# A gated linear attention with a cosine-gated MLP on one core: the last four first-layer tiles as three one-pass products

## The chip, the cores and the metric

The kernel runs on one core of one Trainium2 chip. The metric is the device time of one execution in microseconds; the median over runs is what counts. Five engines take part: TensorE (PE: matmuls, PEld: weight loads), VectorE (DVE), ScalarE (ACT), GpSimd (POOL) and SyncE (SP), which issues most DMAs.

## The reference

```python
# q, k, v, a_re, a_im: (4, 8, 768, 48);  w_in: (384, 2048);  w_out: (2048, 384)
mag = np.sqrt(a_re * a_re + a_im * a_im)
scale = np.minimum(mag, 0.999) / (mag + 1e-06)
a_re_n, a_im_n = (a_re * scale, a_im * scale)
for t in range(S):                      # a complex gate, one per head and channel
    new_re = ar * S_re - ai * S_im
    new_im = ar * S_im + ai * S_re
    S_re, S_im = (new_re + kv, new_im)  # kv: outer product of k and v of step t
    y[:, :, t] = np.einsum('bhd,bhde->bhe', q[:, :, t], S_re)
x = y.transpose(0, 2, 1, 3).reshape(3072, 384)
h = x @ w_in
out = (h * np.cos(h)) @ w_out
```

All of it is float32.

## The kernel before

The 3072 steps are 24 chunks of 128; two chunks make a group, so there are 12 groups (`NG`), three to a batch. `fast_path` turns the recurrence into sums within a chunk: logarithms of the gates are summed by a matmul (`lgs`, exponentials of which scale k and q), angles likewise (`phs`), and the scaled keys and queries are multiplied by cosine and sine of the phase. Scores (`sc`), masked by `causal` into `atm`, meet v and the state carried from the chunk before (`yp`); the state itself comes from `sp`. The result goes through DRAM and comes back as `xT`, 384 rows in three blocks by 256 steps.

For one group n the main loop hands these parts to `weave`, which sorts them by a place between 0 and 1 given with each part:

- `logs(n + 1)`: `log_steps`, ScalarE and VectorE in turn: squares of re and im, logarithms, exponentials, ending in `hi` and `lo`, the two halves of the logarithm that `lgs` multiplies (`prods`, `p_powers`).
- `chunks(n)`: `f_scores`, `f_state`, `f_out` for both chunks.
- `prods(n + 1)`: `lgs`, the arc tangent, `g_split` (a `lo` of the angle), `p_apply`.
- `products(n - 1, ...)`: the second layer of the group before. It is a 2x2 block product done with seven products instead of eight (`seventh`, Strassen's way in Winograd's form); `mixed` makes the four left-hand sums s1 to s4 from the gates, `quarters` those of w_out.
- `phases(n + 1)` and `keys(n + 1)`: `phs`, sine and cosine (`g_trig`), the four products into `ks` and `qs` (`g_stack`), and the turn of both (`f_transpose`): VectorE transposes 32x32 blocks into `tr`, SyncE moves them to DRAM (`moved`) and back (`kT`, `qT`).
- `first(n)`: the first layer, eight tiles of 256 hidden columns (`mm1`). A tile is six products of 128x128 weights by 256 steps in float32, each issued as two matmul rows; ScalarE then takes the sine of the sum (a cosine by its bias) and the square of the sum with its largest value kept (`junk`, a check for range), and VectorE multiplies sum and cosine (`gate`).

Everything on TensorE and most of ScalarE's functions stand in the order in which they are written (`chain` ties each to the one before; `behind` puts one instruction after another without a wait). The other instructions of VectorE, ScalarE and SyncE are placed by the scheduler of the Tile layer. PSUM has five buffers "a" and three for the layers: `hp`, the sum of a first-layer tile, takes "m", "m", "acc" in turn, which `op` and `sum` of the second layer use as well.

Products of two `float32r` operands are issued as one matmul row each, those of float32 as two. `upper_half` uses the type already for `lgs` and `phs`: `hi` by a copy to that type, `lo` by what is left.

Of the kernel before, what the change touches and what calls it, by code (L numbers as in the profile page):

```python
# [487 lines left out]
def fast_path(ctx, tc, q, k, v, a_re, a_im, moe_w_in, moe_w_out, out, least, odd, wide,  # L488
# [12 lines left out]
    G = 2  # L501
# [94 lines left out]
    w_in = wts.tile([C, DF // 256, ND, 256], F32)  # L596
# [4 lines left out]
    def weight_parts():  # L601
        wi = moe_w_in.rearrange("(c p) f -> p c f", p=C)
        wo = moe_w_out.rearrange("(j p) e -> p j e", p=C)
        return ([(w_in[:, i], wi[:, :, ts(i, W)]) for i in range(DF // W)],
                [(w_out[:, ds(j, 2)], wo[:, ds(j, 2)]) for j in range(0, NJ, 2)])
# [20 lines left out]
    def fetched(src):  # L626
        _, a, b = src.shape
        raw = stage["pool"].tile([C, a, b], I64, tag="raw", name="raw", bufs=stage["bufs"])
# [103 lines left out]
    def log_steps(g, i, n):  # L732
# [4 lines left out]
        if i == 0:  # L737
            if g == 0:
                x["sin"] = temp("tan", 2)
            for name in "lg", "tan", "rs", "mag":  # L740
                x[name] = temp(name, 2 if name == "tan" else 1)
        m2, sq, rs, mag = (cut(x[name], i, n) for name in ("lg", "tan", "rs", "mag"))
# [57 lines left out]
    def p_powers(g, i):  # L800

        x = X[g]
        if i == 0:
            x["P"], x["Q"] = x["lg"], temp("Q")
# [91 lines left out]
    def g_trig(g, i, n):  # L896
        x = X[g]
        if i == 0:
            x["cos"] = temp("rs")
            if g:  # L900
# [3 lines left out]
        vector.tensor_scalar(out=cs.bitcast(U32), in0=ph.bitcast(U32),  # L904
                                scalar1=0x7FFFFFFF, scalar2=None, op0=ALU.bitwise_and)
        special(out=sn, in_=ph, func=AF.Sin, scale=TWO_PI)
        special(out=cs, in_=cs, func=AF.Sin, scale=-TWO_PI, bias=half_pi_b)

    def g_stack(g, i, n):
        x = X[g]  # L910
        if i == 0:
            for name in "ks", "qs":
                x[name] = gt.tile([C, G * H, 2, D], F32, tag=name, name=name)
        for name, product in ("ks", "Q"), ("qs", "mag"):
            for a, trig in enumerate(("cos", "sin")):
                vector.tensor_tensor(
                    out=x[name][:, ds(i * H, n * H), a],
                    in0=cut(x[product], i, n).rearrange("p (x d) -> p x d", d=D),
                    in1=cut(x[trig], i, n).rearrange("p (x d) -> p x d", d=D), op=ALU.mult)

    def f_transpose(g, i, n, name):


        if i == 0:
            X[g][name] = ft.tile([D2, G * H, Q4, 32] if name == "kT" else [D2, Q4, G * H, 32], F32,
                                 tag=name, name=name, bufs=1)
        tr = ft.tile([C, NB, n * H, 32], F32, tag="tr", name="tr")
        turn = vector.transpose(out=tr, in_=X[g][name[0] + "s"][:, ds(i * H, n * H)].rearrange(
            "p x a d -> p x (a d)").rearrange("p x (r b) -> p b x r", b=NB))
        if name == "qT" and "gated" in X[g - 1]:  # L930
# [27 lines left out]
    def f_scores(n, hh):  # L958
        y = Y[n]
        if hh == 0:  # L960
            y["atm"] = ft.tile([C, H, C], F32, tag="atm", name="atm")
# [99 lines left out]
    def mm1_sums(g, jp, i=None):  # L1061
# [9 lines left out]
        ps = x["hp"][jp]  # L1071
        lo, n = (0, G) if i is None else (i, 1)
# [605 lines left out]
```

## Time and profile before

| | |
|---|---|
| time, median of 3 runs | 655.62 us (655.18 to 656.74) |
| span of the profiled execution | 651.2 us |
| the profiled execution's own time | the page gives the span alone; 4.4 us lie between it and the median |
| busy: PE, DVE, ACT, POOL | 641.0, 492.0, 392.8, 30.9 us |
| granted TensorE clock | 1.000 over the span |
| first-layer tiles, `hp` | 1176 matmul rows, 252.5 us busy |
| gate: sine, square, product | 96 each, 687, 591, 684 ns |
| DMA traffic | 94.90 MB, mean 146 GB/s |

In the rows of the profile L687 is the line of `matmul`, L676 that of the wrapper through which most VectorE and ScalarE calls go, L707 that of `special` (ScalarE functions with a table). In a timeline row stand start and duration in us, engine, line, operation, output<-inputs, shapes and count, and in brackets the idle time ahead with what ended it. In the chain of work each row is a start, a duration and what ran. Rows of TensorE end some time after the next begins, since matmuls overlap; the pace is read from starts.

### The profile page before, as it was taken

How to read it: one execution, taken by the hardware profiler on the slowest of the kernel's cores; microseconds unless marked ns; L12 is line 12 of the kernel's file. 1: busy time of each engine (PE TensorE's matmuls, PEld its weight loads, DVE VectorE, ACT ScalarE, POOL GpSimd, SP SyncE). 2: the span in 40 equal slices, each digit the busy share in tenths (PEclk: the TensorE clock that was granted, in tenths of full speed). 3: DMA queues.
4: the chain of work that ended last, by engine and by line, in shares of the span. 5: the costliest groups of instructions: out<-in, count | busy, mean ns of one | idle time of the engine just before them, and what ended most of it. 6: DMA issues, size and time to landing. Idle time of an engine off the chain costs nothing.

```text
span 651.2 us, 10758 instructions
## 1 busy us (share of the span) xinstructions
PE 641.0 (98%) x4075; PEld 576.4 (89%) x4075; DVE 492.0 (76%) x799; ACT 392.8 (60%) x726; POOL 30.9 (5%) x53
## 2 busy tenths in 40 slices
PE   8999999999999999999999999999999999999997
PEld 6888877777999999899899899899899999999996
DVE  6999989888687688786787787876877878862251
ACT  7898687284583593494494485485576476433330
POOL 4010200000000000010010010000000000000000
PEclk9999999999999999999999999999999999999999
DMA  9968755727627656747738737836836843363001
GB/s 249 244 179 203 225 164 123 170 62 182 146 49 182 158 146 148 194 110 167 209 82 191 204 85 167 205 96 151 226 105 146 219 123 98 112 134 120 25 1 31
DMA packets 232920, 94.90 MB, mean 146 GB/s; under 512 B 208701, under 2 KB 221246, under 8 KB 232858
## 3 DMA queue, kind: packets, MB, share of 16 engines
q1 hardware_dynamic: 225320, 68.51, 45.3%
q0 software_dynamic: 5824, 25.50, 11.7%
q8 instruction: 34, 0.56, 0.4%
q10 hardware_dynamic: 1714, 0.11, 0.2%
q14 instruction: 28, 0.23, 0.1%
HBM read 69.28 MB, written 24.81 MB: 144 GB/s over the span
## 4 chain that ended last, share of the span: by engine, by line
PE 92%; ACT 4%; DVE 3%; DMA 0%; issue 0%; SPq 0%; DVEq 0%
PE hp L687 38%; PE op L687 18%; PE sum L687 16%; PE sc L687 6%; PE yp L687 6%; PE sp L687 4%; PE phs L687 2%; PE lgs L687 1%; ACT tan L707 1%; PE yr L687 1%; PE tp L948 1%; ACT rs L707 1%; ACT lg L707 1%; ACT L703 1%; DVE mag L676 1%; DVE atm L676 1%
## 5 line engine op out<-in xcount | busy, mean ns | idle before, releaser
L687 PE MATMUL hp<-xT,w_in 128*128 128x256 f32 (+1 forms) x1176 | 252.5, 375 | 0.0
L687 PEld LDWEIGHTS hp<-xT,w_in 128*128 128x128 f32 x1176 | 219.6, 190 | 30.2 <-issue 0.2
L707 ACT ACTIVATE gate<-hp,half_pi_b 128x512 f32<-128x512 f32 x96 | 66.0, 687 | 118.5 <-PE hp L687 118.5
L687 PE MATMUL op<-w_out,gate 128*128 128x192 f32 (+1 forms) x448 | 100.7, 374 | 0.0
L676 DVE TENSOR_TENSOR gate<-hp,gate 128x512 f32<-128x512 f32 x96 | 65.7, 684 | 45.8 <-ACT junk L676 45.7
L687 PEld LDWEIGHTS op<-w_out,gate 128*128 128x128 f32 x448 | 75.9, 190 | 16.9 <-issue 2.0
L676 ACT ACTIVATE junk<-hp 128x512 bf16<-128x512 f32 x96 | 56.7, 591 | 0.0
L687 PE MATMUL sum<-t_s,s 128*128 128x192 f32 x320 | 56.3, 329 | 0.0
L687 PEld LDWEIGHTS sum<-t_s,s 128*128 128x128 f32 x320 | 52.1, 190 | 1.5 <-issue 1.5
L676 DVE TENSOR_TENSOR atm<-sc,causal 128x512 f32<-128x512 f32 x48 | 32.9, 689 | 23.4 <-PE sc L687 23.4
L687 PEld LDWEIGHTS sc<-qT,kT 96*128 96x128 f32 x384 | 47.4, 192 | 2.3 <-issue 0.6
L687 PE MATMUL sc<-qT,kT 96*128 96x128 f32 x384 | 49.0, 276 | 0.2 <-ACT qT L676 0.2
L676 ACT ACTIVATE ot<-sum 128x192 f32<-128x192 f32 x39 | 12.6, 322 | 53.7 <-PE sum L687 53.4
L676 DVE SCALAR_TENSOR_TENSOR ot<-op,ot 128x192 f32<-128x192 f32 x40 | 13.3, 354 | 38.0 <-PE op L687 36.4
L687 PE MATMUL yp<-atm,v 128*48 128x128 f32 x352 | 33.6, 277 | 0.9 <-ACT Q L707 0.6
L703 ACT ACT_TABLE_LOAD x24 | 30.8, 1283 | 1.2 <-PEq L1662 0.7
L676 ACT COPY yT<-yp 48x512 f32<-48x512 f32 x44 | 25.3, 574 | 7.4 <-PE yp L687 7.0
L687 PE MATMUL yp<-qT,state 96*48 96x128 f32 x304 | 29.7, 272 | 0.0
L687 PE MATMUL sum<-w_out,gate 128*128 128x192 f32 x160 | 29.7, 329 | 0.0
L687 PE MATMUL sp<-v,ks 128*96 128x48 f32 x320 | 29.7, 245 | 0.0
L687 PEld LDWEIGHTS sp<-v,ks 128*96 128x96 f32 x320 | 29.6, 165 | 0.0
L676 ACT CAST tan<-phs 128x384 int32<-128x384 f32 x24 | 11.4, 480 | 29.4 <-PE phs L687 29.4
(147 smaller groups left out, 987.4 us busy)
## 6 DMA issues: line engine op xcount, KB each, us to landing
moved<-tr SPq DMA_DIRECT2D x20, 768.0 KB
raw<-in_moe_w_in_dram POOLq DMA_DIRECT2D x16, 768.0 KB, 5.1
raw<-in_moe_w_out_dram POOLq DMA_DIRECT2D x16, 768.0 KB, 4.6
kT<-moved SPq DMA_DIRECT2D x40, 192.0 KB
qT<-moved SPq DMA_DIRECT2D x10, 768.0 KB
k<-in_k_dram SPq DMA_DIRECT2D x24, 192.0 KB
q<-in_q_dram SPq DMA_DIRECT2D x24, 192.0 KB
v<-in_v_dram SPq DMA_DIRECT2D x24, 192.0 KB
```

Of the source, the lines that this page charges most:

```text
L676: ins = getattr(self.engine, op)(**kw)
L687: chain(nc.tensor.matmul(out, **kw), "tensor")
L703: chain(nc.scalar.preload_act_table_set(table))
L707: chain(nc.scalar.activation(func=func, **kw))
L948: chain(nc.tensor.transpose(ps[:, h], X[g][name[0] + "s"][:, x0 + h].rearrange("p a d -> p (a d)"), ident), "tensor")
```

## The change

For four of the eight tiles of a group (jp = 4 from group 2 on, 5 and 6 from group 3, 7 from group 4) the six float32 products are replaced. Weights and x are cut into an upper part of 12 bits and a lower rest (scaled by 4096 for the weights): w = wh + wl, x = xh + xl. With a third pair, wx = wh - 4096 wl and xx = xh - 4096 xl in the terms of the code, three one-pass sums of six products each give the tile: wh xh and wl xl go into `hp`, wx xx into a second PSUM tile `hb` from pool "a". ScalarE copies `hb`, scaled, into the tile's gate buffer (`cross_out`), VectorE adds that into `hp` (`whole_sum`), and sine, square and product follow with a factor 1 + 1/4096. Per group x is cut by `x_halves` (`cut`, `xl`, `xx` on VectorE, `xh` on ScalarE), the weights once each by `halves`.

Other edits come with it: first-layer tiles run in the order 0 to 7 instead of 0, 4, 1, 5 and so on; `mixed` makes s1 alone, and s3, s2 and s4 are made later, in place in the gates, by `mixed_again`; the phases stand one product sooner; `g_trig` takes the absolute value on ScalarE from group 2 on; `g_stack` does the sine products first; buffers are shared to make room (Q and mag in one tile "pair" that also takes the turned queries, `qs` with `atm`, the raw weights of the late range check with `tr`); and the range checks of the weights stand in 0.1 to 0.56 instead of 0.1 to 0.9.

```diff
     def g_trig(g, i, n):
...
-        vector.tensor_scalar(out=cs.bitcast(U32), in0=ph.bitcast(U32),
-                                scalar1=0x7FFFFFFF, scalar2=None, op0=ALU.bitwise_and)
-        special(out=sn, in_=ph, func=AF.Sin, scale=TWO_PI)
+        if g >= PEG:
+            special(out=sn, in_=ph, func=AF.Sin, scale=TWO_PI)
+            scalar.activation(out=cs, in_=ph, func=AF.Abs)
...
+    def three_halves(jp, wl, wx):
+        cut_ = ft.tile([C, ND, 256], F32, tag="tr", name="cut", bufs=1)
+        w = w_in[jp]
+        vector.tensor_scalar(out=cut_.bitcast(U32), in0=w.bitcast(U32), scalar1=UPPER,
+                             scalar2=None, op0=ALU.bitwise_and)
+        yield
+        vector.tensor_tensor(out=wl, in0=w, in1=cut_, op=ALU.subtract)
+        w_in[jp] = wts.tile([C, ND, 256], F32R, tag=f"w_in{jp}", name="wh", bufs=1)
+        scalar.copy(out=w_in[jp], in_=cut_)
+        yield
+        vector.scalar_tensor_tensor(out=wx, in0=wl.bitcast(F32), scalar=-SHIFT, in1=cut_,
+                                    op0=ALU.mult, op1=ALU.add)
+        scalar.mul(out=wl, in_=wl.bitcast(F32), mul=SHIFT)
...
+        def lower():
+            scalar.copy(out=x["xh"], in_=x["cut"])
+            low = vector.tensor_tensor(out=x["xl"], in0=all_of(), in1=x["cut"], op=ALU.subtract)
+            if g + 1 < NG:
+                behind(low, X[g + 1]["qT turn"])
+        def apart():
+            vector.scalar_tensor_tensor(out=x["xx"], in0=x["xl"].bitcast(F32), scalar=-SHIFT,
+                                        in1=x["cut"], op0=ALU.mult, op1=ALU.add)
...
+    def mm1_three(g, jp, ps):
+        x.setdefault("hb", {})[jp] = pb = pa.tile([C, 2, G * C], F32, tag="a", name="hb")
...
+        for part in (straight, crossed) if k == 0 else (crossed, straight):
+            part()
...
+    def cross_out(g, jp):
+        scalar.mul(out=new_gate(g, jp), in_=X[g]["hb"].pop(jp), mul=-1.0 / (SHIFT + 1.0))
+    def whole_sum(g, jp):
+        ps = X[g]["hp"][jp]
+        behind(vector.tensor_tensor(out=ps, in0=ps, in1=X[g]["gate"][jp], op=ALU.add),
+               X[g]["product"])
...
     def mm1(g, jp):
         mm1_sums(g, jp)
-        mm1_gate(g, jp)
+        if three(g, jp):
+            cross_out(g, jp)
+            if three(g, jp - 1):
+                mm1_gate(g, jp - 1)
+            whole_sum(g, jp)
+        if not three(g, jp) or jp == NJ // 2 - 1 or not three(g, jp + 1):
+            mm1_gate(g, jp)
...
+    FROM, UPPER, SHIFT = {4: 2, 5: 3, 6: 3, 7: 4}, 0xFFFFF000, 4096.0
...
-        weave((mixes(n - 1, 2, 4), 0.0, 0.12), (logs(n + 1), 0.0, 0.02), (chunks(n), 0.0, 0.36),
+        weave((mixes(n - 1, 2, 4), 0.0, 0.08), (logs(n + 1), 0.0, 0.02), (chunks(n), 0.0, 0.36),
...
-              (phases(n + 1), *((0.472, 0.476) if n == PLAIN else (0.516, 0.524))),
-              (keys(n + 1), *((0.5, 0.62) if n == PLAIN else (0.53, 0.64))),
+              (phases(n + 1), *((0.472, 0.476) if plain else (0.476, 0.484))),
+              (turned_keys[0:1], 0.5, 0.5), (split[0:1] if n == NG - 1 else [], 0.525, 0.525), (turned_keys[1:2], 0.53, 0.53),
+              (turned_keys[2:3], 0.56, 0.56), (turned_keys[3:4], 0.6, 0.6), (split[1:2], 0.61, 0.61),
+              (split[2:3], 0.65, 0.65), (last_quarter() if plain else [], 0.9, 1.0), (first(n), 0.56, 1.0),
```

How this moves instructions, at the three places that matter below. First TensorE, from the phases to the end of a group's first layer. Before:

```order
L687 MATMUL phs<-lo,exact 128x384
L687 MATMUL sum<-w_out,s 128x192 x8
L687 MATMUL hp<-xT,w_in 128x256 x48
L687 MATMUL sc<-qT,kT 128x128 x4
L687 MATMUL sum<-w_out,gate 128x192 x4
```

Now, up to the second of the four tiles (`hb` x12 is the crossed sum of two tiles, one behind the other):

```order
L689 MATMUL phs<-lo,exact 128x384
L689 MATMUL op<-w_out,gate 128x192 x8
L689 MATMUL sum<-w_out,gate 128x192 x8
L689 MATMUL hp<-xT,w_in 128x256 x24
L689 MATMUL hp<-xh,wh 128x256 x3
L689 MATMUL hp<-xl,wl 128x256 x3
L689 MATMUL hp<-xh,wh 128x256 x3
L689 MATMUL hp<-xl,wl 128x256 x3
L689 MATMUL hb<-xx,wx 128x256 x12
```

Two products of the second layer now stand between the phases and the first layer, where one stood, and half of the first layer is one-pass products.

Second VectorE, from the turn of the keys (`tr<-ks`) on, in the groups from 4 on. Before:

```order
L676 STREAM_TRANSPOSE tr<-ks 128x1536
L676 SCALAR_TENSOR_TENSOR least<-end,least 96x16
L676 TENSOR_TENSOR gate<-hp,gate 128x512
L676 STREAM_TRANSPOSE tr<-qs 128x1536
L676 TENSOR_TENSOR gate<-hp,gate 128x512
L676 TENSOR_TENSOR s<-gate 128x256
```

Now:

```order
L678 TENSOR_SCALAR cut<-xT 128x768
L678 TENSOR_TENSOR gate<-hp,gate 128x512
L678 STREAM_TRANSPOSE tr<-qs 128x1536
L678 TENSOR_TENSOR xl<-xT,cut 128x768
L678 TENSOR_TENSOR gate<-hp,gate 128x512
L678 SCALAR_TENSOR_TENSOR xx<-xl,cut 128x768
L678 TENSOR_TENSOR gate<-hp,gate 128x512 x2
L678 TENSOR_TENSOR hp<-hp,gate 128x512
L678 SCALAR_TENSOR_TENSOR gate<-hp,gate 128x512
L678 TENSOR_TENSOR hp<-hp,gate 128x512
```

The cut of x stands ahead of tile 0's product, the two other passes over x behind the turn of the queries, and each tile from 4 on has an addition into `hp`, behind the product of the tile before.

Third ScalarE in the second half of the first layer and behind it. Before, each tile is a sine and a square, and then come the squares of the next logarithms:

```order
L707 ACTIVATE gate<-hp,half_pi_b 128x512
L676 ACTIVATE junk,wide<-hp 128x512
L749 ACTIVATE lg<-re 128x768
L749 ACTIVATE tan<-im 128x768
L703 ACT_TABLE_LOAD
```

Now, from the last of the four scaled copies of `hb` on:

```order
L678 ACTIVATE gate<-hb 128x512
L709 ACTIVATE gate<-hp,half_pi_b 128x512
L678 ACTIVATE junk,wide<-hp 128x512
L709 ACTIVATE gate<-hp,half_pi_b 128x512
L678 ACTIVATE junk,wide<-hp 128x512
L753 ACTIVATE lg<-re 128x768
```

Each copy stands one tile ahead of the sine that comes next, and the squares of the next group's logarithms still follow the last tile's square.

More of the change, by code (lines that the diff above doesn't have):

```diff
@@ L594, in fast_path @@
     nc.vector.memset(least, 1.0)
-    w_in = wts.tile([C, DF // 256, ND, 256], F32)
+    w_in = [wts.tile([C, ND, 256], F32, tag=f"w_in{i}", name="w_in", bufs=1)
+            for i in range(DF // 256)]
     w_out = wts.tile([C, NJ, DM], F32)
@@ L739, in log_steps @@
                 x["sin"] = temp("tan", 2)
-            for name in "lg", "tan", "rs", "mag":
+            for name in "lg", "tan", "rs":
                 x[name] = temp(name, 2 if name == "tan" else 1)
+            both = gt.tile([C, 2, G * DM], F32, tag="pair", name="pair")
+            x["Q"], x["mag"] = both[:, 0], both[:, 1]
         m2, sq, rs, mag = (cut(x[name], i, n) for name in ("lg", "tan", "rs", "mag"))
@@ L1211, in mixes, with mixes_again, stepwise @@
         return [lambda p=p: mixed(g, p) for p in range(lo, hi)] if g >= PLAIN else []
+    def mixes_again(g, name):
+        return [lambda p=p: mixed_again(g, p, name) for p in range(HJ // 2)] if g >= PLAIN else []
+    def stepwise(part, count):
+        part = iter(part)
+        return [lambda: next(part, None) for _ in range(count)]
     def weave(*parts):
```

130 lines of the change are left out of this document (98 added, 32 removed).

## The prediction

> **What bounds the kernel now.** I read the page first: busy shares, the chain that ended last, the costliest groups.
>
> ```profile
> PE 641.0 (98%) x4075; PEld 576.4 (89%) x4075; DVE 492.0 (76%) x799; ACT 392.8 (60%) x726; POOL 30.9 (5%) x53
> ...
> PE 92%; ACT 4%; DVE 3%; DMA 0%; issue 0%; SPq 0%; DVEq 0%
> ...
> L676 DVE TENSOR_TENSOR gate<-hp,gate 128x512 f32<-128x512 f32 x96 | 65.7, 684 | 45.8 <-ACT junk L676 45.7
> ```
> TensorE is busy for 98% of the span and makes 92% of the chain, so a microsecond taken from it can be worth a microsecond. The third row shows the followers' habit: VectorE's gate product idles almost only for ScalarE's square (`junk`), not for the sine that it multiplies by.
>
> Then the chain in order of time, which gives the beat: one stage of eight first-layer tiles (`hp`) per group.
>
> ```profile
> 204.33 20.72 PE hp L687 x96
> ...
> 255.53 20.72 PE hp L687 x96
> ...
> 305.77 20.72 PE hp L687 x96
> ...
> 353.49 2.60 PE sum L687 x16
> ...
> 356.09 20.72 PE hp L687 x96
> ...
> 407.30 20.72 PE hp L687 x96
> ...
> 457.54 20.72 PE hp L687 x96
> ...
> 507.86 20.72 PE hp L687 x96
> ...
> 559.54 20.72 PE hp L687 x96
> ...
> 607.62 20.72 PE hp L687 x96
> ```
> A stage takes 20.72, and the starts lie 51.2, 50.24, 50.32, 51.21, 50.24, 50.32, 51.68 and 48.08 apart. Only the last interval holds no chain of logarithms for a later group. 353.49 is one 16-row product, 2.60.
>
> Whether the chains beside TensorE would follow a faster stage is read where they meet it, at the `lgs` products (sums of logarithms). Matmul rows of two periods, then VectorE's `lo`, the operand of `lgs`, in the first:
>
> ```profile
> 339.26 0.33 PE L687 MATMUL lgs<-lo,exact 128*128 128x384 f32 x1
> ```
> ```profile
> 355.93 20.88 PE L687 MATMUL hp<-xT,w_in 128*128 128x256 f32 x96
> ...
> 390.47 0.34 PE L687 MATMUL lgs<-lo,exact 128*128 128x384 f32 x1
> ```
> ```profile
> 338.07 0.95 DVE L676 SCALAR_TENSOR_TENSOR lo<-lg,hi 128x768 fp32r<-128x768 f32 x1
> ```
> With S the stage's start (355.93; 305.61 in the period before, 0.16 ahead of the chain's row), `lo` ends at 339.02 and TensorE uses it at 339.26: slack 0.24. In the other period `lo` (388.39, below) ends at 389.34 against 390.47: slack 1.1. So TensorE looks like the bound, but a second chain, from the stage's last gate through the logarithms to `lgs`, is 0.2 to 1.1 us behind it. A gain on TensorE beyond that is kept only if this chain comes earlier too.
>
> **The change, part by part.** All times count from S.
>
> TensorE. A tile is now 12 rows; 96 rows take 20.72, so 2.59 per tile and 0.216 per row (two passes of 256 columns). It becomes 18 one-pass products of 256 columns. The trace has one-pass products of 384 and 512 columns:
>
> ```profile
> 352.14 0.47 PE L687 MATMUL phs<-hi,exact 128*128 128x384 f32 x1
> ...
> 352.45 0.34 PE L687 MATMUL phs<-lo,exact 128*128 128x384 f32 x1
> ...
> 352.98 0.34 PE L687 MATMUL phs<-lo,alls 128*128 128x384 f32 x1
> ```
> ```profile
> 18.25 1.62 PE L687 MATMUL busy<-idle 128*128 128x512 f32 x5
> ...
> 18.25 2.54 PE L687 MATMUL busy<-idle 128*128 128x512 f32 x9
> ```
> Three starts in 0.53 are 0.177 for 384 columns; four in 0.92 are 0.230 for 512. The line through both gives 0.124 at 256, proportion 0.118; I take 0.121. It is at least 0.108 (half of a two-pass row of the same width) and at most 0.177. So a tile takes 2.18 and saves 0.41. The table FROM gives 10+9+9+8 = 36 tiles: 14.8 us of matmul time (0.108: 23; 0.177: a loss of 21). The step from 352.14 to 352.45 shows some 0.13 more where one-pass follows two-pass products, so a full stage ends at 10.36+0.13+8.71 = 19.2 instead of 20.72.
>
> The Trainium skill, page "TensorE: Matmul & The Clock Gate", section "Back-to-back issue gap", gives N/2.4 + 2.5 ns, which is 109 ns at 256 columns; it also gives 162 and 216 at 384 and 512, where this trace has 177 and 230, so the rows decide. By the page a tile would save 0.63 and all of them 22.5.
>
> Phases one product sooner. They start 2.60 earlier, at 352.14-355.93-2.6 = -6.4. The absolute value moves from VectorE to ScalarE in front of the cosine (768 columns, about 0.8); VectorE takes both sine stacks first. The turn of the keys then starts at about 1.1 instead of 3.14:
>
> ```profile
> 345.46 0.94 DVE L676 SCALAR_TENSOR_TENSOR lo<-tan,hi 128x768 fp32r<-128x768 f32 x1
> ...
> 359.07 2.25 DVE L676 STREAM_TRANSPOSE tr<-ks 128x1536 f32<-128x1536 f32 x1
> ...
> 361.28 0.69 DVE L676 TENSOR_TENSOR gate<-hp,gate 128x512 f32<-128x512 f32 x1
> ...
> 361.88 2.25 DVE L676 STREAM_TRANSPOSE tr<-qs 128x1536 f32<-128x1536 f32 x1
> ...
> 365.54 0.42 DVE L676 TENSOR_TENSOR gate<-gate 128x256 f32<-128x256 f32 x1
> ...
> 370.38 0.69 DVE L676 TENSOR_TENSOR gate<-hp,gate 128x512 f32<-128x512 f32 x1 [0.19 <-ACT junk L676]
> ...
> 387.52 0.95 DVE L676 TENSOR_TENSOR mag<-mag,tan 128x768 f32<-128x768 f32 x1
> ...
> 388.39 0.95 DVE L676 SCALAR_TENSOR_TENSOR lo<-lg,hi 128x768 fp32r<-128x768 f32 x1
> ```
> But ScalarE's queue now has the copy `xh` ahead of tile 0's sine, and `xh` needs `cut`, which VectorE runs after that turn: turn 1.1 to 3.3, `cut` (taken as 0.5, at most the 0.9 of a 768-column `mag`) to 3.9, `xh` (768 columns, as 378.01 below) to 4.7, sine and square 1.3, product of tile 0 at 6.0 (before: 361.28, 5.35), and behind it in VectorE's queue the turn of the queries from 6.6 to 8.7 (before 5.95 to 8.2). `xl`, product 1, `xx`, product 2 end at 9.6, 10.2, 11.1 and 11.7 (0.6 to 0.9 each). Tile 4 needs `xl` and the PSUM buffer that product 1 frees at 10.36: covered by 0.1 only; if VectorE is late by 0.5 the stage is late by 0.4.
>
> SyncE's queue turns the queries through DRAM; its last issue and the end of the traffic:
>
> ```profile
> 369.98 1.25 SPq L938 DMA_DIRECT2D qT<-moved  x1
> ```
> ```profile
> 374.00:375.00 1.00, 1.00 1.07 229
> 375.00:376.00 1.00, 1.00 0.22 55
> 376.00:377.00 1.00, 1.00 0.00 0
> ```
> The traffic ends at about 375.2, which is 19.3, and scores began at 20.7. The turn ends 0.5 later, so the queries land at about 19.8 while TensorE is ready at 19.2: a new wait of 0.6 to 0.8 per group, outside the logarithms' chain.
>
> The gates of the one-pass tiles. Each adds a scaled copy (ScalarE), an addition into PSUM (VectorE) and a loop: the addition of tile j stands behind the product of tile j-1 in VectorE's queue.
>
> ```profile
> 343.33 1.17 ACT L676 COPY yT<-yp 48x512 f32<-48x512 f32 x2
> ...
> 358.72 0.69 ACT L707 ACTIVATE gate<-hp,half_pi_b 128x512 f32<-128x512 f32 x1 [2.20 <-PE hp L687]
> ...
> 369.08 0.69 ACT L707 ACTIVATE gate<-hp,half_pi_b 128x512 f32<-128x512 f32 x1 [1.26 <-PE hp L687]
> ...
> 376.85 0.69 ACT L707 ACTIVATE gate<-hp,half_pi_b 128x512 f32<-128x512 f32 x1 [1.32 <-PE hp L687]
> ...
> 378.01 0.84 ACT L749 ACTIVATE lg<-re 128x768 f32<-128x768 f32 x1
> ...
> 385.94 0.84 ACT L707 ACTIVATE tan<-tan 128x768 f32<-128x768 f32 x1
> ```
> Per tile: addition to sine 0.73 (the 0.69 of a 512-column product and a hand-over), sine to product 1.30 (369.08 to 370.38, since the product waits for the square), product to next addition 0.60 (361.28 to 361.88): 2.63. That is more than a tile's 2.18, so this loop and not TensorE paces tiles 4 to 7. (If the product waited for the sine alone it would be 2.1; the rows exclude that.) The crossed product of tile 4 ends at 10.49+18x0.121 = 12.67; ScalarE sees it 0.2 later (358.72 against 355.93+2.59); the copy takes 0.58 (two `yT` in 1.17), so the addition starts at 13.45, sine 4 at 14.2, and sine 7 at 14.2+3x2.63 = 22.1. Before, it was 376.85, 20.92. The last tile's followers are 1.2 later though its matmuls are 1.5 earlier. Buffers still come free in time: tile 7 needs product 4 (16.1) at 16.9 or later.
>
> The logarithms behind them. ScalarE squares `re` right after the last gate (378.01, 22.08 before; now 23.2). From there to the last exponential (385.94) took 7.93; one `yT` copy of 0.58 now stands inside: 31.7. Then 0.84, `mag` 0.87, `lo` 0.95 and hand-overs of 0.1 give 34.5; VectorE's queue (the mixes are four per pair as before, but three of them stand here now, 0.42 each by 365.54, and two score masks) can add up to 0.4. I take 34.6. TensorE took `lo` at 339.26-305.61 = 33.65 in the short periods and at 390.47-355.93 = 34.54 in the long ones. So `lgs` comes 0.95 later in a short period and 0.06 later in a long one, and TensorE, which could be there at 32.1 or 33.0, waits 1.6 to 2.5 for `lo`. Behind `lgs` the order up to the next stage is TensorE's own; phases need a `lo` of their own, which ended 7.1 after TensorE took the first (345.46+0.94-339.26), and now stand 352.14-339.26-2.6 = 10.3 after it, so their being sooner costs nothing.
>
> Sum. Starts 204.33 to 559.54 are seven periods, three long and four short: 3x0.06+4x0.95 = 4.0. The first stage has one tile of the kind and gains the slack, 0.2. The period without logarithms (559.54 to 607.62) keeps 1.5 less the query wait of 0.7: 0.8. The end keeps 1.5, less 0.9, since the second product needs tile 7's gate at 19.2+2.6+1.3 = 23.1 and gets it at 24.0: 0.6. Splitting four weight tiles is three VectorE and two ScalarE passes of 768 columns each, 16 us in all; they stand among the gates of the stage, where VectorE idles for `junk`; uncovered a part of up to 3 shows, I take 0.5. Together 4.0-0.2-0.8-0.6+0.5 = +2.9. The profiled span is 651.2, the median of the runs 655.62; the 4.4 around the span stay. So 658.5.
>
> **The rivals.**
> 1. The chain of logarithms keeps up and TensorE stays the bound. For it: VectorE idles 45.7 us for `junk`, and turns start 2 us sooner. Against it: the loop of 2.63 and a slack of 0.24. It needs the last sine at 19.4 or earlier, i.e. a loop near 1.8. Time: 655.6-14.8+2 (query waits partly hidden) = 643. By the 109 ns of the Trainium skill's section above it would be near 635.
> 2. Nothing measurable moves: the loop is 2.45 (an addition into PSUM shorter than a product), the last sine and `lo` 0.5 earlier, at 34.1, so short periods lose 0.45 and long ones gain 0.45, the ends gain 1.6 and splitting costs 0.5: 655.
> 3. One-pass products do not pay: at 0.177 the stage ends at 23.2, 2.5 later than before, and ten stages make 655.6+21 = 677. It decides from 0.144 on (2.59/18). Against it: both pairs of rows lie under 0.125.
>
> **How the numbers follow.** Runs differ by up to 0.24%, so 0.3% (2 us) is about what can be told from no change. The forecast gets 0.48, its own range 654 to 664 (`lo` 0.5 earlier or 0.7 later in seven periods, splitting 0 to 3); rival 1 gets 0.26, rival 2 0.2, rival 3 0.06. Faster than 653.6: rival 1 and a fifth of rival 2, 0.30. Slower than 657.6: 0.4 of the forecast and rival 3, 0.46. The rest, 0.24, is the same. The range of 8 in 10 leaves out rival 3 and the better half of rival 1: 645 to 666.
>
> **What would show it.** Right: matmuls `hp<-xh,wh` start 0.12 apart; a stage lasts 19 to 20; the last sine of a stage comes 22 after S; TensorE waits for VectorE's `lo` at `lgs` by 1.5 to 2.5 in nearly every group and for the queries at `sc` by 0.6; periods from 204 to 560 are all near 51.2, no longer 50.3 and 51.2. Wrong: no wait at `lgs` and periods near 49.6 (rival 1); a pitch above 0.14 (rival 3); a stage that waits at tile 4 for `xl` or a buffer makes it slower than I say; a loop below 2.4 makes it faster.

## The result, and the profile after

The changed kernel takes 673.67 us (median of four runs, 671.89 to 675.50) against 655.49 us before: a ratio of 1.0282, 95% interval 1.0252 to 1.0312. The forecast was 658.5, and its range ended at 666. The profiled execution took 675.03, its span 673.2, so 22.0 us more than the span of before; its mean granted clock is 0.993 against 1.000.

Busy time, from the head of the page of the changed kernel, and then what TensorE waited for over the span (us in total, times, longest), from its table of waits:

```profile
PE 635.2 (94%) x4291; PEld 573.7 (85%) x4291; DVE 534.6 (79%) x867; ACT 433.5 (64%) x790; POOL 30.7 (5%) x53
```
```profile
PE sc L689 <- DMA qT<-moved: 10.1, 5, 3.2
PE lgs L689 <- DVE lo L678: 7.3, 8, 1.4
PE hp L689 <- DVE gate L678: 4.0, 5, 1.4
```
TensorE is busy for 5.8 us less, where 14.8 was forecast; spells at half clock, below, are a part of the difference (6.8 us of them, so 3.4 at most). The new idle time stands mainly at three places: scores wait for the queries, `lgs` waits for `lo`, and first-layer tiles wait for a PSUM buffer that a gate frees.

One stage, S = 370.68, shows what came as forecast. TensorE's rows (start, duration, names, shape, count, and idle time with its releaser in brackets):

```profile
382.65 1.59 PE L689 MATMUL hb<-xx,wx 128*128 128x256 f32 x12
384.09 0.52 PE L689 MATMUL hp<-xh,wh 128*128 128x256 f32 x3
...
389.43 0.52 PE L689 MATMUL hp<-xl,wl 128*128 128x256 f32 x3
391.54 1.13 PE L689 MATMUL sc<-qT,kT 96*128 96x128 f32 x8 [1.59 <-DMA qT<-moved]
...
405.18 0.42 PE L689 MATMUL lgs<-hi,exact 128*128 128x384 f32 x1
405.88 0.44 PE L689 MATMUL lgs<-lo,exact 128*128 128x384 f32 x1 [0.29 <-DVE lo L678]
```
Twelve one-pass rows start 382.65 to 384.09, 0.120 each (forecast 0.121). The last tile ends near S+19.1 (forecast 19.2). But the scores begin at 391.54 = S+20.9, and the `lgs` products follow 13.64 after them with 0.29 more of waiting for `lo`.

ScalarE and VectorE in the same stage:

```profile
374.76 0.83 ACT L678 CAST xh<-cut 128x768 fp32r<-128x768 f32 x1 [3.55 <-DVE cut L678]
375.50 0.68 ACT L709 ACTIVATE gate<-hp,half_pi_b 128x512 f32<-128x512 f32 x1
...
384.94 0.69 ACT L709 ACTIVATE gate<-hp,half_pi_b 128x512 f32<-128x512 f32 x1
...
387.63 0.69 ACT L709 ACTIVATE gate<-hp,half_pi_b 128x512 f32<-128x512 f32 x1 [0.61 <-DVE hp L678]
...
390.32 0.69 ACT L709 ACTIVATE gate<-hp,half_pi_b 128x512 f32<-128x512 f32 x1 [0.94 <-DVE hp L678]
...
393.00 0.69 ACT L709 ACTIVATE gate<-hp,half_pi_b 128x512 f32<-128x512 f32 x1 [1.42 <-DVE hp L678]
```
```profile
376.79 0.69 DVE L678 TENSOR_TENSOR gate<-hp,gate 128x512 f32<-128x512 f32 x1 [2.12 <-ACT junk L678]
377.39 2.25 DVE L678 STREAM_TRANSPOSE tr<-qs 128x1536 f32<-128x1536 f32 x1
```
The copy `xh` stands ahead of tile 0's sine, which starts as soon as the copy is done; VectorE idles 2.12 for the square behind it and only then makes product 0 and, at S+6.71, the query turn (forecast 6.6). The sines of tiles 5 to 7 come 2.69 apart (forecast 2.63), the last at S+22.3 (forecast 22.1). All of this is as worked out.

What is not: the queries. Stretches of a quarter of a us (length, busy time of PE, PEld, DVE, ACT and POOL, granted clock, DMA share, GB/s):

```profile
390.25:390.50 0.25, 0.00 (x0) 0.00 (x0) 0.25 (x1) 0.18 (x1) 0.00 (x0) 1.00 0.41 98
390.50:390.75 0.25, 0.00 (x0) 0.00 (x0) 0.22 (x2) 0.25 (x1) 0.00 (x0) 1.00 0.17 41
390.75:391.00 0.25, 0.00 (x0) 0.00 (x0) 0.25 (x1) 0.25 (x2) 0.00 (x0) 1.00 0.00 0
```
The traffic ends at about 390.8, S+20.1 (forecast 19.8), and the product that reads the queries starts 0.75 us after that. In some other periods it is later still, and in two of them the clock then falls (the scores' row, and stretches of one us):

```profile
338.10 1.19 PE L689 MATMUL sc<-qT,kT 96*128 96x128 f32 x8 [3.22 <-DMA qT<-moved]
```
```profile
338.00:339.00 1.00, 0.90 (x8) 0.91 (x9) 0.16 (x1) 1.00 (x3) 0.00 (x0) 1.00 0.00 0
339.00:340.00 1.00, 1.00 (x6) 1.00 (x5) 0.67 (x2) 1.00 (x4) 0.00 (x0) 0.55 0.00 0
340.00:341.00 1.00, 1.00 (x4) 1.00 (x4) 0.74 (x4) 0.98 (x2) 0.00 (x0) 0.50 0.00 0
341.00:342.00 1.00, 1.00 (x5) 1.00 (x5) 0.75 (x3) 0.96 (x1) 0.17 (x1) 0.50 0.00 0
342.00:343.00 1.00, 1.00 (x10) 1.00 (x8) 0.31 (x1) 0.00 (x0) 0.62 (x1) 0.75 0.00 0
```
TensorE stood idle for 3.22 ahead of 338.10; from 339.1 the granted clock is one half for 3.4 us. A second such spell follows a wait of only 1.72 (443.63), while the wait of 1.95 ahead of 497.37 is followed by none. Before the change no stretch was under 1.00.

In a table, S counted from the first `hp` row of a stage, all read from rows of TensorE and ScalarE as above; the period goes to the next S:

| S after | first `sc` at S+ | `lgs` takes `lo` at S+ | last sine at S+ | period | period before |
|---|---|---|---|---|---|
| 155.49 | 22.96 | 36.80 | 23.97 | 53.57 | 50.32 |
| 209.06 | 21.34 | 35.36 | 23.35 | 53.85 | 51.21 |
| 262.91 | 21.62 | 35.91 | 23.39 | 52.69 | 50.24 |
| 315.60 | 22.50 | 38.32 | 22.33 | 55.08 | 50.32 |
| 370.68 | 20.86 | 35.20 | 22.32 | 51.96 | 51.21 |
| 422.64 | 20.99 | 36.69 | 22.33 | 53.47 | 50.23 |
| 476.11 | 21.26 | 35.39 | 22.36 | 52.17 | 50.32 |
| 528.28 | 20.88 | 34.58 | 22.35 | 52.73 | 51.69 |
| 581.01 | 19.03 | none | 22.13 | 47.10 | 48.07 |

S comes 1.65 later already at the first row, the eight periods with logarithms cost 20.0, the ninth gives 0.97 back, and the end costs 1.3: 22.0. Only the ninth keeps what the one-pass products save: it has no logarithms beside it, and its query turn starts at S+4.7.

### The profile page after: what moved, and what is told of

Same layout as the page of the kernel before. It is cut to its first block, busy times and chain, and to the rows that moved or that the text cites. A ratio compares the mean times of both kernels' runs of the same rounds, so it can differ in the third digit from the quotient of the medians.

```text
span 673.2 us, 11371 instructions
## 1 busy us (share of the span) xinstructions
PE 635.2 (94%) x4291; PEld 573.7 (85%) x4291; DVE 534.6 (79%) x867; ACT 433.5 (64%) x790; POOL 30.7 (5%) x53
## 5 line engine op out<-in xcount | busy, mean ns | idle before, releaser
L689 PE MATMUL hp<-xT,w_in 128*128 128x256 f32 (+1 forms) x744 | 160.3, 373 | 4.4 <-DVE gate L678 2.4
L689 PEld LDWEIGHTS hp<-xT,w_in 128*128 128x128 f32 x744 | 137.1, 190 | 25.0 <-DMA xT<-x 2.9
L689 PE MATMUL sc<-qT,kT 96*128 96x128 f32 x384 | 50.7, 281 | 11.6 <-DMA qT<-moved 10.1
L689 PE MATMUL sum<-w_out,gate 128*128 128x192 f32 x304 | 56.9, 337 | 0.0
L689 PEld LDWEIGHTS sum<-w_out,gate 128*128 128x128 f32 x304 | 51.1, 196 | 0.0
L689 PE MATMUL hp<-xh,wh 128*128 128x256 f32 x216 | 38.5, 287 | 1.5 <-DVE gate L678 1.5
L689 PE MATMUL hp<-xl,wl 128*128 128x256 f32 x216 | 37.3, 281 | 0.0
L689 PEld LDWEIGHTS hp<-xh,wh 128*128 128x128 f32 x216 | 30.9, 189 | 4.5 <-DVE gate L678 4.4
L678 DVE TENSOR_TENSOR gate<-gate 128x256 f32<-128x256 f32 x80 | 32.7, 419 | 2.3 <-PE op L689 1.4
L678 DVE TENSOR_TENSOR hp<-hp,gate 128x512 f32<-128x512 f32 x36 | 24.9, 693 | 9.1 <-ACT gate L678 9.1
L689 PEld LDWEIGHTS hp<-xl,wl 128*128 128x128 f32 x216 | 30.6, 188 | 0.0
```

The costliest lines, as they stand in the source:

```text
L678: ins = getattr(self.engine, op)(**kw)
L689: chain(nc.tensor.matmul(out, **kw), "tensor")
```

## The experiments

Theory A is that late queries are what lengthens the periods, rival B that it is the loop of the last tiles and the logarithms behind it (the forecast), rival C that it is the rest of the change, or, later, the slow clock.

**Without the one-pass tiles.**

```diff
-    FROM, UPPER, SHIFT = {4: 2, 5: 3, 6: 3, 7: 4}, 0xFFFFF000, 4096.0
+    FROM, UPPER, SHIFT = {}, 0xFFFFF000, 4096.0
...
-        split = x_halves(n)
-        if n + 1 < NG:
+        split = ()
+        if split and n + 1 < NG:
```

> The changed kernel without its one-pass tiles and without the splitting of x and of the weights: all eight tiles of the first layer in two passes as before, but with the new order of the tiles, the new places of the mixes, of the key and query turns and of the phases, the pools and the separate weight tiles. Theory A: TensorE needs its 20.7 us for the stage again, the query turn has no copy ahead of it, and the periods are those of before: 652 to 658 us. Rival C, the other moves cost: 660 us or more.

Measured 654.64, ratio 0.9996 (0.9973 to 1.0018). New order, mixes, pools and phases cost nothing by themselves; the whole loss comes with the one-pass tiles and the splitting.

**The kernel before, with its query turn later.**

```diff
-        x.setdefault("gated", gated)
+        if "one" in x:
+            x.setdefault("gated", gated)
+        x["one"] = gated
...
-              (keys(n + 1), *((0.5, 0.62) if n == PLAIN else (0.53, 0.64))),
+              (turned_keys[0:3], *((0.5, 0.59) if n == PLAIN else (0.53, 0.6125))), (turned_keys[3:4], 0.66, 0.66),
```

> The kernel before, with the query turn behind the second product of the stage instead of the first, some 2.0 to 2.7 us later; nothing else is changed. Theory A: the queries had only about 0.3 us to spare, so the scores wait 1.7 to 2.4 us in each of 8 periods: 668 to 676 us. Rival B: the slack up to the end of the DMA traffic (1.4 us) counts and the wait is taken back at lgs: 655 to 662 us.

Measured 669.21, ratio 1.0201 (1.0142 to 1.0260). VectorE's turn in that run, where it stood at 361.88 = S+5.95 before:

```profile
370.97 0.69 DVE L676 TENSOR_TENSOR gate<-hp,gate 128x512 f32<-128x512 f32 x1 [1.24 <-ACT junk L676]
371.58 2.25 DVE L676 STREAM_TRANSPOSE tr<-qs 128x1536 f32<-128x1536 f32 x1
```
With S = 364.22 it starts at S+7.36, only 1.41 later, and not 2.0 to 2.7 as expected. Still the scores begin on average 1.0 later and the mean of the eight periods rises from 50.69 to 52.48. So the queries had little slack in the kernel before, not the 1.4 us between S+19.3, where the prediction has the end of their traffic, and the scores at S+20.7.

**The query turn first.**

```diff
-              (turned_keys[2:3], 0.56, 0.56), (turned_keys[3:4], 0.6, 0.6), (split[1:2], 0.61, 0.61),
+              (turned_keys[2:3], 0.56, 0.56), (turned_keys[3:4], 0.57, 0.57), (split[1:2], 0.61, 0.61),
```

> The changed kernel, with the query turn put ahead of the first product of the stage. The turn then follows the key turn directly (from 377.4 to about 373.9 in the stage at 370.68), so the queries land some 3.5 us sooner. Theory A, the queries' arrival is what lengthens the periods: the scores start at S+19.1 instead of S+20.9, the wait for qT at the scores goes, and the time falls by 8 x 1.8 plus the half-clock spells: 652 to 660 us. Rival B, the forecast: the loop of addition, sine, square and product and the logarithms behind it set the period; the wait only moves from the scores to lgs, whose last piece comes at S+34.5 as before, and the periods stay at 51.2 or more: 664 to 672 us. Rival C, the cost lies in the rest of the change: 670 us or more.

Measured 684.09, ratio 1.0446 (1.0407 to 1.0485): slower than the changed kernel. Only rival C's number allows that, and its reason is excluded by the run without one-pass tiles. Its waits, and ScalarE in the stage at S = 533.72:

```profile
PE hp L689 <- DVE gate L678: 8.9, 8, 2.2
PE lgs L689 <- ACT hi L730: 8.0, 6, 1.8
PE lgs L689 <- DVE lo L678: 7.6, 7, 1.6
```
```profile
539.69 0.83 ACT L678 CAST xh<-cut 128x768 fp32r<-128x768 f32 x1 [5.44 <-DVE least L678]
540.43 0.68 ACT L709 ACTIVATE gate<-hp,half_pi_b 128x512 f32<-128x512 f32 x1
...
556.92 0.69 ACT L709 ACTIVATE gate<-hp,half_pi_b 128x512 f32<-128x512 f32 x1 [1.42 <-DVE hp L678]
```
No wait for the queries is left. But `cut` now stands behind both turns in VectorE's queue, `xh` idles ScalarE for 5.44 and starts at S+6.0, tile 0's sine at S+6.7; the first gates are late, tiles wait for their PSUM buffers, the last sine moves to S+23.2, and `lgs` waits for both of its operands. The wait moves to `lgs` as rival B says, and grows. Since the late first gates are a second change, this alone does not refute theory A; the run with the copy later, below, has the queries early without them.

**The squares behind the products.** In the built program the product of a tile waits for ScalarE's square, which reads the same PSUM tile and is written first.

```diff
     def mm1_gate(g, jp):
+        ps = X[g]["hp"][jp]
         gate_sine(g, jp)
         gate_product(g, jp)
+        if three(g, jp):
+            gate_square(g, jp, ps, (1.0 + 1.0 / SHIFT) / in_scale)
```

> The changed kernel, with the square of each one-pass tile written behind its product, so that the loop of the last tiles is addition, sine, product (0.60 + 0.68 + 0.69, about 2.1 us a tile) instead of 2.69. The last sine comes at about S+20.9 instead of S+22.3. Theory A: the scores wait for the queries all the same, and the time stays within 3 us of 673. Rival B: the periods lose the 1.4 us of the last sine eight times: 660 to 664 us.

Measured 666.57, ratio 1.0170 (1.0118 to 1.0222): 7 us of the loss, between the two expectations. The last sine comes at S+20.9 to S+21.2 in five of the seven stages from the second on. The queries are still late, and the wait for `lo` is less than half of what it was:

```profile
PE sc L689 <- DMA qT<-moved: 8.2, 6, 2.2
PE lgs L689 <- DVE lo L678: 3.0, 4, 1.4
```

**The copy of x later.**

```diff
-            scalar.copy(out=x["xh"], in_=x["cut"])
+            high = scalar.copy(out=x["xh"], in_=x["cut"])
+            behind(high, x["square"])
```

> The changed kernel, with the copy of x's upper half in ScalarE's queue behind the first tile's sine and square instead of ahead of them. The first product and the query turn behind it come 0.75 us sooner, the scores start at about S+20.1 instead of S+20.9. Two bounds (the queries at 20.9, and last sine 22.3 with the logarithms behind it): the periods lose 0.5 to 0.8 us each, 664 to 669 us. If the copy is not what delays the queries: 672 to 675 us.

Measured 671.67, ratio 1.0242 (1.0191 to 1.0294): less than expected, and hardly apart from the change itself. VectorE in the stage at S = 316.23:

```profile
320.32 0.69 DVE L678 TENSOR_TENSOR gate<-hp,gate 128x512 f32<-128x512 f32 x1
320.93 2.26 DVE L678 STREAM_TRANSPOSE tr<-qs 128x1536 f32<-128x1536 f32 x1
```
The turn starts at S+4.70 instead of S+6.71, so the copy cost it 2.0 us, not 0.75. In five of eight stages the scores start at S+19.4 or earlier. Yet TensorE then waits 8.9 us for `lo` and 5.8 for `hi` at `lgs` instead: again the wait moves.

The small gain hides a larger one. The eight periods together are 7.0 us shorter than in the changed kernel, but the first stage starts 2.8 later, with a half-clock spell at 142.4 ahead of it. At like granted clock the edit gives about 6 us, by single runs (666.61 against 672.32 at 0.994); two of its four runs were at 0.978 and took some 674. So late queries do cost, though less than theory A says.

**Key reads ahead of the queries' write.**

```diff
+        if name == "qT":
+            behind(put, X[g]["kT read"])
```

> The changed kernel, with the four reads of the keys ahead of the write of the queries in SyncE's queue. The key reads then wait for the keys' own write alone, and of the queries only one write and one read are left behind the turn, so they land about 1.5 us sooner and the scores start at S+19.4. Theory A, the queue is what makes the queries late: 655 to 661 us. Rival B, the logarithms behind the last sine (S+22.3) take over: 660 to 666 us. If the queue's order is not what counts: 671 to 675 us.

Measured 695.19, ratio 1.0618 (1.0570 to 1.0667); the expectation was wrong in sign. SyncE's queue in the stage at S = 267.71:

```profile
271.91 0.33 SPq L946 DMA_DIRECT2D moved<-tr  x1
275.34 3.82 SPq L951 DMA_DIRECT2D kT<-moved  x4
279.25 1.14 SPq L946 DMA_DIRECT2D moved<-tr  x1
283.81 0.33 SPq L953 DMA_DIRECT2D qT<-moved  x1
```
The key reads are issued 3.4 after the write they wait for, the query read 4.6 after its own, and the two round trips now stand one behind the other. In the changed kernel both writes go first and the key reads pass behind them without a wait of that size. But this is not the whole of the 21.5 us: over the seven stages from the second on the scores start only 0.5 later than in the changed kernel. VectorE's order, which the scheduler of the Tile layer sets, moved too. The first mask of the scores (`atm`) now stands behind the logarithms' `lg`, at about S+25.8 in most stages instead of S+22.5 to S+23.7, and TensorE's `yp` products wait 13.6 us in all for masks, where the changed kernel has no such wait. So the run does not show what the order in SyncE's queue alone costs.

**Turn first and copy later, together.** The edits of both, and:

```diff
             if g + 1 < NG:
                 behind(low, X[g + 1]["qT turn"])
+            behind(low, x["product"])
```

> The changed kernel with the query turn ahead of the first product, and with the copy of x's upper half and its lower half behind the first tile's square and product. The queries are in time and the first products are not held up, so TensorE does not wait for a PSUM buffer. What is left is the loop of the last tiles with its last sine at S+22.3: by rival B lo comes at S+34.8, TensorE waits 1.5 to 2 us at lgs, and the periods are 51.2 to 51.8: 657 to 663 us. If the loop did not matter, TensorE is the bound with periods of 49.5: 644 to 648 us. If the first tiles still stall as in the run with the query turn alone: over 670 us.

Measured 669.20, ratio 1.0184 (1.0140 to 1.0228). (The profiled execution took 674.31.) TensorE in two places, then stretches between them:

```profile
345.81 0.44 PE L689 MATMUL lgs<-hi,exact 128*128 128x384 f32 x1 [1.43 <-ACT hi L730]
347.55 0.69 PE L689 MATMUL lgs<-lo,exact 128*128 128x384 f32 x1 [1.29 <-DVE lo L678]
```
```profile
345.00:346.00 1.00, 0.18 (x1) 0.19 (x1) 1.00 (x4) 0.97 (x3) 0.00 (x0) 1.00 0.02 3
346.00:347.00 1.00, 0.26 (x1) 0.00 (x0) 1.00 (x2) 0.97 (x2) 0.00 (x0) 0.67 0.88 172
347.00:348.00 1.00, 0.45 (x1) 0.45 (x2) 1.00 (x2) 0.49 (x2) 0.22 (x1) 0.50 0.85 160
348.00:349.00 1.00, 1.00 (x5) 0.56 (x6) 1.00 (x3) 0.73 (x2) 0.54 (x1) 0.50 0.30 59
```
This is the forecast's machine by itself: the scores start at S+18.9, the last sine comes at S+22.1, `lo` is taken at S+34.4 to S+35.1 in seven of eight periods (forecast 34.6), and where the clock stays up the periods are 51.8 to 52.0 (forecast 51.2). But in five of eight periods the two waits at `lgs` are followed by a half-clock spell of 3.4 or 6.8 us, and these periods take 53.3 to 55.8. The four runs of this one kernel order themselves by granted clock: 663.61 at 0.995, 669.07 at 0.987, 669.34 at 0.985, 674.31 at 0.976. With few spells this kernel is thus at 663.6, just over the 657 to 663 of rival B.

**TensorE kept busy at that place.**

```diff
+        if g > PLAIN and i == 0:
+            for _ in range(8):
+                matmul(ps[:, 0:256], lhsT=w_in[0][:, 0, 0:C], rhs=w_in[0][:, 0],
+                       start=True, stop=True)
         summed_up(ps, g, i, "lg", upto[0])
```

> The run with the query turn first and the copy of x later, with eight 128x256 matmuls (1.73 us) of no use put into TensorE's queue just ahead of the logarithms' first sum, where it waited 0.5 to 1.9 us for hi and then 0.7 to 1.5 us for lo. Their result is overwritten. Theory C, the half-clock spells behind these waits cost what the waits alone do not: with TensorE kept busy the granted clock stays at 1.00, all periods fall to the 51.9 us that the undisturbed stages of that run have, and the time to 656 to 660 us, faster for having more work. Rival: the waits alone count, the added matmuls at best fill them: 667 to 672 us, and over 672 if they push the sums back.

Measured 675.80, ratio 1.0292 (1.0272 to 1.0312), at a granted clock of 1.00: over 672, as the rival has it for sums that are pushed back. The filling was twice as long as meant:

```profile
403.13 3.69 PE L689 MATMUL lgs<-w_in 128*128 128x256 f32 x16
```
With four instead of eight:

> The run with the query turn first and the copy of x later, with four 128x256 matmuls of no use ahead of the logarithms' first sum instead of eight. The trace of the run with eight showed 16 records in 3.3 us, 0.21 each (two passes a matmul), twice what had been worked out: it kept the clock at 1.00 but pushed the sums back by more than the wait it filled. Four take 1.7 us, within the waits for hi and lo of 2.0 to 2.8 us. Theory C, half-clock spells are a loss of their own: clock 1.00, periods 51.7 to 52.3, 657 to 662 us. Rival, only the waits count: 667 to 671 us as without them.

Measured 666.37, ratio 1.0172 (1.0140 to 1.0205), clock 0.995 to 1.000; the profiled execution has no spell and periods of 51.4 to 53.2. Between the two expectations, and not clear of the kernel without filling, whose four runs took 663.61 to 674.31: the filling is not shown to gain anything. `lo` is still taken at S+34.9 on average.

That a spell is a loss of its own is seen in single periods instead. In the run with the copy later, TensorE's own order from `lo` to the next stage takes 16.8 us without a spell (51.89 less 35.13 at S = 316.23) and 19.7 with 6.83 us at half clock in it (54.66 less 34.97 at S = 261.56). By this measure the 6.8 us at half clock of the changed kernel are worth some 3 of its 18 us, an estimate.

**All three edits** (turn first, copy later, squares behind products).

> As the run with the query turn first and the copy of x later, and with the square of each one-pass tile behind its product: queries in time, first tiles free, last sine at about S+20.9 or sooner. Two bounds: both are moved ahead of TensorE's 19.1 and 33, the periods come to 49.5 to 50.2 and the time to 644 to 651 us, less than before. If a third wait is behind these two (the additions of the matching products, the phases): 655 us or more, and the trace names it.

Measured 656.39, ratio 1.0023 (1.0003 to 1.0042): 17 of the 18 us are back, but nothing is gained. The scores start at S+19.0, the last sine comes at S+20.9 and `lo` at S+33. TensorE still waits 5.5 us for `lo` and 3.3 for `xT` in all. The longest period, 53.5, is that of the stage at S = 359.95; VectorE, SyncE and TensorE there:

```profile
399.70 0.56 DVE L678 TENSOR_SCALAR raw<-raw 128x768 uint32<-128x768 uint32 x1 [2.16 <-DMA raw<-in_moe_w_in_dram]
400.30 0.62 DVE L678 SCALAR_TENSOR_TENSOR tan<-tan,carry 32x384 f32<-32x384 f32 x1
```
```profile
404.71 0.24 SPq L839 DMA_DIRECT2D row<-lg  x1
405.05 0.81 SPq L1062 DMA_DIRECT2D x<-yT  x2
```
```profile
413.44 0.89 PE L689 MATMUL hp<-xT,w_in 128*128 128x256 f32 x3 [1.78 <-DMA xT<-x]
```
A range check of the weights waits 2.16 for its DMA in VectorE's queue, ahead of the angle's work. Behind it VectorE ends `lg` at 404.64, SyncE issues `row<-lg` at 404.71, and only then the write `x<-yT`, though the last copy into `yT` had ended at 398.66; the next stage waits 1.78 for `xT`. By these rows the two waits are one chain, which was not tried. So a third wait stands close behind the two that were removed.

**The same without moving the query turn.**

> The changed kernel with its four one-pass tiles and the query turn where it was, behind the first product; only the copy of x's upper half comes later and the squares stand behind the products. If the copy ahead of the first sine is what made the queries late, the turn's own place does not matter and the time is that of the run with all three edits: 655 to 660 us. If the turn's place matters too: 662 to 667 us.

Measured 658.01, ratio 1.0034 (1.0013 to 1.0055), within the interval of all three: with the squares behind the products, the turn's own place matters little; the copy ahead of tile 0's sine was what made it late.

**Three one-pass tiles.**

```diff
-    FROM, UPPER, SHIFT = {4: 2, 5: 3, 6: 3, 7: 4}, 0xFFFFF000, 4096.0
+    FROM, UPPER, SHIFT = {4: 2, 5: 3, 6: 3}, 0xFFFFF000, 4096.0
```

Alone in the changed kernel:

> The changed kernel with three one-pass tiles (4, 5, 6) instead of four and nothing else changed: the copy ahead of the first sine, the squares ahead of the products. The queries arrive at S+20.9 as before, TensorE now ends its tiles at S+19.5 and waits 1.4 us instead of 1.8; lo comes 1 us sooner and no longer ahead of nothing: periods 51.2 to 51.8, 657 to 664 us. If the fourth tile alone was the fault (the last loop): 648 to 653 us. If the number of tiles hardly matters while the queries are late: 668 to 672 us.

Measured 659.58, ratio 1.0062 (1.0038 to 1.0086): the fourth tile alone cost 14 us, although it saves TensorE 0.4 a stage; here too the scores start at S+21.1 and the last sine at S+20.9. With all three edits, and with the two that matter:

> As the run with all three edits, but with three one-pass tiles (4, 5, 6) instead of four; the last tile is in two passes and needs no addition. TensorE saves 1.2 us a stage instead of 1.6, the last sine follows the last matmul directly (S+19.7 instead of S+20.9), and lo comes at S+32.5 ahead of TensorE. If the loop of the last tiles is what is left of the loss, the periods are 49.3 to 50.3: 643 to 651 us. If other waits are (the weights' guard in VectorE's queue, xT): 653 to 657 us.

> As the run before in this call (the copy later, the squares behind the products, the turn behind the first product), with three one-pass tiles (4, 5, 6). If the turn's place does not matter, the time is that of the run with three tiles and all three edits: 648 to 652 us. If it does: 654 to 658 us.

Measured 649.89, ratio 0.9925 (0.9901 to 0.9949), and 650.33, ratio 0.9909 (0.9873 to 0.9945): both beat the kernel before, by 0.75% and 0.91%. The waits of the first:

```profile
PE lgs L689 <- DVE lo L678: 2.9, 5, 1.4
PE yp L689 <- DVE atm L678: 2.5, 5, 0.8
```
The last tile in two passes needs no addition, so its sine starts 0.26 after the last matmuls (S+19.63 against S+19.37), and the wait for `lo` falls from 5.5 with four tiles and the same edits to 2.9.

Ten of the kernels in one view. The middle columns are from the profiled executions: means over the seven stages from the second on, the period over eight, and the time at half clock between 150 and 640. The last is the median of all runs, so it need not fit the columns ahead of it:

| kernel | `sc` at S+ | last sine | `lo` taken | period | at half clock, us | time |
|---|---|---|---|---|---|---|
| before | 20.7 | 20.9 | 33.8 | 50.7 | 0 | 655.5 |
| changed | 21.4 | 22.6 | 35.9 | 53.2 | 6.8 | 673.7 |
| turn first | 20.2 | 23.3 | 35.8 | 54.2 | 23.9 | 684.1 |
| copy later | 19.3 | 22.1 | 34.6 | 52.3 | 10.2 | 671.7 |
| squares behind | 21.0 | 21.3 | 35.1 | 52.6 | 10.2 | 666.6 |
| turn first, copy later | 19.2 | 22.1 | 34.6 | 53.4 | 30.7 | 669.2 |
| the same, filled by four | 19.1 | 22.1 | 34.9 | 52.3 | 0 | 666.4 |
| all three | 19.1 | 20.8 | 33.1 | 51.4 | 3.4 | 656.4 |
| three tiles only | 21.1 | 20.9 | 34.4 | 51.7 | 3.4 | 659.6 |
| three tiles, all three | 19.5 | 19.7 | 32.8 | 50.4 | 0 | 649.9 |

## Why the prediction was wrong

What held: the pitch, the end of the stage, the time of the query turn, the loop of 2.63 and the last sine, each within 0.25 us of the trace. Rival 1 (TensorE stays the bound) and rival 3 (one-pass does not pay) fell as argued, and the loop of 2.45 that rival 2 needs did not come (2.69). With the queries in time, `lo` is taken where it was forecast, at S+34.6 on average. The side was right, slower, and the loop was rightly named as part of what sets it: with the squares behind the products, which shortens it, 7 of the 18 us are back, and without the fourth tile 14.

The step that failed is the query wait, "a new wait of 0.6 to 0.8 per group, outside the logarithms' chain". Measured, TensorE waits 1.57 to 3.22 for the queries in the five stages from S = 315.60 to 528.28, and the scores start at S+21.3 there on average, where the tiles end at 19.1. Two terms of the sum were wrong. The first is the end of the traffic in the kernel before. The prediction puts it at 375.2 (S+19.3), from a mean share of 0.22 over one us; quarters of a us show that it runs on until 375.5, S+19.6:

```profile
375.25:375.50 0.25, 0.25 (x3) 0.22 (x2) 0.00 (x0) 0.25 (x2) 0.00 (x0) 1.00 0.11 25
375.50:375.75 0.25, 0.25 (x3) 0.23 (x2) 0.19 (x1) 0.03 (x1) 0.00 (x0) 1.00 0.00 0
```
With 0.5 added for the later turn this gives the S+20.1 that was measured at S = 370.68. The second, larger term was put at nothing: from the last packet to the product that reads the queries, 0.75 us pass. Together they make S+20.9 of S+19.8. The same two terms shrink the slack of the kernel before from 1.4 to about 0.4, an estimate (20.72 less 19.6 less 0.75), which fits the run with the later turn.

"Outside the logarithms' chain" held in part. In the stage shown `lo` is taken at S+35.2, and so it is in the run with the copy later, where the queries are in time (S+35.16 at S = 368.11); the periods are 51.96 and 51.94. Late queries were dear elsewhere: in the first two periods, which cost 5.9 more than before, 1.7 with the copy later and 1.0 with all three edits, and in the two periods with a spell at half clock, which cost 8.0 more than before.

The slack of 0.2 to 1.1 at `lgs` was that of the two periods read. In three of the eight there was none: in the first of them `lo` ends at 288.77 and TensorE, idle for 0.15, takes it at 288.83.

The spell is a term that the sum does not have: it let a wait cost its length. In the run that isolates the forecast's mechanism (turn first, copy later), periods without a spell are 0.6 to 0.8 above the forecast and those with one 2.1 to 4.6. The Trainium skill, page "TensorE: Matmul & The Clock Gate", section "Part 1: The HAM clock gate", tells of a window of 3413 ns, not tied to the kernel's start, after which an idle TensorE runs at half rate. The length of the spells here, 3.4 us or twice that, agrees; that a whole idle window is needed does not, since a wait of 1.72 was followed by one.

The sum had +0.5 for splitting the weights and -0.2 for the first stage. In the trace the first stage already starts 1.65 later. Without one-pass tiles that start is 154.02, 0.2 from before, so this goes with the splitting; how it divides between VectorE's passes and buffers was not tried. The ninth period (0.97 kept, forecast 0.8) was right; the end cost 1.3 where 0.6 was to be kept, and why stays open.

The runs do not divide the 18 us into parts that add up. The copy alone gives 2 in the median (about 6 at like clock), the squares alone 7, both together 15.7, the fourth tile alone 14: queries and loop meet TensorE in the same period, and removing one leaves the other.

## What to carry to other kernels

Where an engine at 98% is made faster, list every chain that meets it in the period with the time at which it arrives, and take the gain only up to the second latest; here the queries, `lo` and `xT` stood within about 2 us of TensorE. The arrival of a transfer is when the consumer has been seen to start on it after a wait, not when the traffic ends (0.75 us earlier here); if no row of the kernel shows such a wait, count its slack as nothing. When a speed-up lengthens the chain behind its own last tile, leave that tile out: with the same other edits three quicker tiles gained 0.8% here where four lost 0.2%.

## What the runs showed of the hardware

- From the end of the queries' DMA traffic to the first product that reads them passed 0.75 us (about 390.8 to 391.54), and from the issue of a write to DRAM to the issue of the read that waits for it 3.4 to 4.6 us (271.91 to 275.34, 279.25 to 283.81).
- The granted clock fell to 0.50 for 3.4 us, or 6.8. In every trace the spells start a whole number of steps of 3.413 us apart (in the changed kernel at 339.09 and 444.91, 31 steps), which suggests that the idle time that falls into one step counts, not the length of a wait alone. In the changed kernel the steps just ahead of the two spells hold 2.42 and 1.72 us of idle; the wait of 1.95 that ends at 497.37 is cut by the bound at 496.1 into 0.7 and 1.3, and no spell followed. Over all traces the step ahead of a spell held 1.2 to 2.4 of idle, and steps with up to 1.8 were followed by none, so no exact threshold is shown.
- In one kernel 0.019 of mean clock went with 10.7 us (663.61 and 674.31).
- A float32 matmul of 256 columns is two records of 0.21 each (eight of them left 16), a one-pass product one record of 0.12.
- Written ahead of the product, ScalarE's square held VectorE's product of the same PSUM tile back; written behind it, the pitch of the last sines fell from 2.69 to 2.51, 2.25 and 2.05 (381.33, 383.83, 386.08 and 388.13 in one stage).
